# Reordering the opening of an attention and Fourier-mix kernel: sums ahead of products, short extra products, one load on another queue, weight conversions at other places

## The chip, the cores and the metric

The kernel runs on one core of a Trainium2 chip. The metric is device time in microseconds (us) of one execution. A core has five engines that matter here, each with its own instruction queue worked off in order: TensorE (PE), VectorE (DVE), ScalarE (ACT), GpSimd (POOL) and SyncE (SP), which here only issues loads and stores (DMAs). ScalarE can issue DMAs too.

## The reference

Eight batches, each with eight heads, a sequence of 576 and 64 elements per head (512 in all). Softmax over the elements of each query and over the sequence of each key; key-value products; queries times these give `x`. Then a Fourier mix, a normalisation and a two-layer MLP of width 2048 with a residual:

```
q_s = softmax(q, axis=-1);  k_s = softmax(k, axis=seq)
kv  = einsum('bhsd,bhse->bhde', k_s, v)
x   = einsum('bhsd,bhde->bhse', q_s, kv)      # joined to (B, S, 512)
u   = x + real(fft(fft(x, axis=seq), axis=512))
un  = (u - mean(u)) / sqrt(var(u) + 1e-6)
out = u + relu(un @ w1) @ w2
```

All inputs are f32, and the weights come as 64-bit words.

## The kernel before

**Batches.** For each batch the keys' exponentials are transposed on TensorE and multiplied with the values into block-diagonal 128x128 blocks (`kvr`). Queries come in tiles of 128 rows. Four such tiles of batch 0 are called A, B, D and C in the opening; the 64 rows of a batch that fill no tile of their own are handled with those of another batch as a "shared" tile `t`. A query tile is exponentiated, transposed (`turn`), copied, and multiplied with `kvr` to give `x`. The mix folds `x` by symmetry (`folded`, L936 to L956, on VectorE), multiplies the folds with tables `ft` (`block`, L988 and L991), then with `cd` (`second`, L1016 and L1019), adds, normalises, transposes (L1096) and lays the result out for the MLP (L1104).

**Stages.** From 0 to 56 us the opening runs attention and mix of batch 0 and the key products of batch 1. From 56.05 us the MLP of batch 0 runs as plain products (`plain`: 16 blocks of four 128x512 products at L1150, then 64 products at L1162). Beside it each piece of weights is converted from its words, in steps called hi, shift, sign, lo and add: two on ScalarE (L368, L369), two on VectorE (L362, L365), one on GpSimd (L370). Eight pairs of pieces per layer are then combined by four subtractions or additions on VectorE (`combine`, L420) and stored, and batch 1's attention, folds and mix are made ready. From 195.69 us on, batches 1 to 7 and the shared rows go through an MLP in Strassen's form (L1224 and after); TensorE bounds that part.

**Order.** Nothing is scheduled by the machine's state. Each step has a time written by hand or computed from a formula, all steps are sorted by it, and each engine gets its instructions in that order. The times are no clock; only their order counts. The opening's times are in the string `OPENING`, where "k03 max" is the maximum of batch 0's fourth block of keys, "k0 last" and "k0 fifth" are the transposes of the keys' last 128 columns and their copy, "t exp0" to "t exp3" are two exponentials each of the shared rows, "A kv" the products of tile A with `kvr`, "b1 times" a block of the mix, "c0 hi" a step of the first conversion. The times of the later steps are at the end of the program, as offsets from `first` (47.8) and from `t`, which is `first + 56`.

**Loads.** `loads_first` issues the loads of the opening. ScalarE issues four loads of shared rows (L264); SP issues four blocks of keys (L274), the first queries (L283), then the four first rows of the shared tile (`shared_firsts`, L267, 8 KB), then values, queries, values, tables, and batch 1's keys and values. Each load has one of eight completion counters, taken in rotation, and waits for the earlier load on its counter to land.

**Sums of exponentials.** Batch 0's query tiles are normalised after the product. In `q_times_kv` four products of 128x8 with a matrix of ones (L874) give the sums, in the same step as the four products with `kvr` (L876); VectorE then adds an epsilon and inverts (L881, L882), and scales the product into `x` (L890).

Of the kernel before, what the change touches and what calls it, by code (L numbers as in the profile page):

```python
# [40 lines left out]
F32 = mybir.dt.float32  # L41
# [5 lines left out]
P = 128  # L47
# [35 lines left out]

DOWN = [(i, f) for n in range(4) for i in (2, 3, 0) for f in range(4 * n, 4 * n + 4)] + [(1, f) for f in range(NF)]
OPENING = """
5.20 k00 max, 6.00 k00 exp, 6.20 k01 max, 6.95 k00 turn, 7.00 k01 exp, 7.20 k02 max, 7.80 k00 four,
7.95 k01 turn, 8.00 t max, 8.30 k02 exp, 8.60 k03 max, 9.06 k01 four, 9.25 k02 turn, 9.56 k03 exp, 10.20 A max,
10.32 t exp0, 10.51 k0 last, 10.80 B max, 10.80 t exp1, 10.95 A less, 11.28 t exp2, 11.40 k0 fifth,
11.76 t exp3, 11.99 B less, 12.00 k0 inverse, 12.12 k03 turn, 12.24 A exp, 12.37 t inverse, 12.74 k02 four,
12.82 k00 kv, 13.24 k03 four, 13.37 t normal, 13.72 A turn, 13.74 B exp, 14.00 C max, 14.17 k01 kv,  # L90
14.32 A copy, 14.60 D max, 14.75 C less, 15.07 B turn, 15.52 t turn, 15.67 B copy, 15.79 D less, 16.10 k02 kv,
16.17 t copy, 16.67 C exp, 16.83 t fold, 17.15 k03 kv, 17.17 D exp, 18.05 C turn, 18.20 k0 scale0,
18.28 t join, 18.50 D turn, 18.65 k0 scale1, 19.10 A kv, 20.10 B kv, 20.25 A inverse, 20.25 D copy,
20.65 A out, 21.10 D kv, 21.25 C copy, 21.27 k10 max, 21.94 B inverse, 22.07 k10 exp, 22.10 C kv,
22.25 D inverse, 22.50 B out, 23.10 k10 turn, 23.12 D out, 23.55 t kv, 23.70 k10 four, 23.74 C inverse,
23.99 tokens1, 24.25 t parts, 24.61 C out, 25.23 columns1, 25.59 tokens0, 26.21 t folds, 26.96 columns0,
27.44 by1, 27.80 by0, 28.28 again0, 28.58 again1, 28.60 c0 hi, 29.08 tokens3, 29.18 b1 times, 29.25 c0 lo,
29.70 tokens2, 30.16 b0 times, 30.32 columns3, 30.38 b1 copies, 30.68 columns2, 31.14 b4 times, 31.16 by2,
31.36 b0 copies, 31.52 by3, 32.00 again2, 32.30 again3, 32.34 b4 copies, 32.80 k13 max, 32.90 b2 times,
33.47 c0 shift, 33.60 k13 exp, 33.88 b3 times, 34.17 c0 sign, 34.36 b2 copies, 34.77 k12 max, 34.86 k13 turn,  # L100
34.89 c0 add, 35.08 b3 copies, 35.44 k11 max, 35.63 k12 exp, 35.78 m1 times, 36.39 k13 four, 36.68 k12 turn,
36.89 m1 copy, 37.13 m0 times, 37.28 k12 four, 37.39 m1 sums, 37.78 k11 exp, 38.29 m1 add0, 38.54 m0 copy,
38.73 k11 turn, 38.89 roots, 38.97 m1 add1, 39.04 m0 sums, 39.18 k1 last, 39.84 k1 inverse, 40.04 s10,
40.19 k11 four, 40.27 m0 add1, 40.69 k1 fifth, 40.79 s11, 41.34 k10 kv, 41.57 m0 add0, 41.69 root1,
42.09 k11 kv, 42.25 scales1, 42.45 s00, 42.60 normal11, 42.84 k12 kv, 43.20 s01, 43.44 turn11, 43.95 normal10,
44.04 k13 kv, 44.10 root0, 44.30 laid11, 44.45 scales0, 44.64 turn10, 44.80 normal00, 44.80 normal01,
45.30 k1 scale0, 45.39 laid10, 45.55 turn01, 45.75 k1 scale1, 46.15 turn00, 46.30 laid01, 46.90 laid00"""
ATT_EPS = 1e-9
# [27 lines left out]
class _Block:  # L136
# [96 lines left out]
    def xshared(self, p):  # L233
        return self.xpart(B, p % 2, p // 2)

    def halves(self):
        return self.work.tile([P, 2 * NN], F32, tag="eo", name="eo", bufs=6)

    def loads_first(self, fetch):
# [45 lines left out]
        def second(r):  # L285
# [282 lines left out]
    def opening(self, fetch, converted):  # L568
# [22 lines left out]
        for n, it in own.items():  # L591
            named(f"{n} max,{n} less,{n} exp", self.q_exp_spread(it))
            named(f"{n} turn,{n} copy", self.q_turn(it))
            named(f"{n} kv,{n} inverse,{n} out", self.q_times_kv(it))
        for name, f in zip(("tokens", "columns", "by", "again"), self.folded(0)):
# [20 lines left out]
        assert not steps, steps  # L616
        return placed

# [242 lines left out]
    def q_times_kv(self, it):  # L861
        nc, (_, b, c, u) = self.nc, it
        box = []

        def times():
            qT, *rec = self.live.pop(it)
            px = self.acc((P, D))
            box.extend([px, *rec])
            if b == 0:
                n = {(0, 0): "bb", (1, 1): "bc", (0, 1): "ba", (1, 0): "bb"}[c, u]  # L870
                t = self.ps.tile([P, 512], F32, tag=n, name=n)
                box.append(t)
                for r in range(NR):
                    nc.tensor.matmul(t[:, 0:H], lhsT=qT[:, r, :], rhs=self.ones[:, r, :], start=r == 0, stop=r == NR - 1)  # L874
            for r in range(NR):
                nc.tensor.matmul(px[:, r * P:(r + 1) * P], lhsT=qT[:, r, :], rhs=self.kvr[b % 2][:, r, :], start=True,  # L876
                                 stop=True)

        def inverse():
            t = self.small.tile([P, H], F32, tag="qrec", name="qrec", bufs=4)  # L880
            nc.vector.tensor_scalar(out=t[:], in0=box[1][:, 0:H], scalar1=ATT_EPS, scalar2=None, op0=ALU.add)  # L881
            nc.vector.reciprocal(t[:], t[:])  # L882
            box[1] = t[:].unsqueeze(2).to_broadcast([P, H, DH])
# [601 lines left out]
def kernel(ctx: ExitStack, tc: tile.TileContext, q, kT, v, w1, w2, ft,  # L1485
# [68 lines left out]
    steps.append((t + 12, lambda: setattr(blk, "spare_words", blk.raws[LATE_WORDS[0]].bitcast(F32))))  # L1554
    steps += [(t + 12 + 4 * i, lambda i=i: blk.load(i)) for i in range(3)] + [(t + 71, lambda: blk.load(3))]
# [8 lines left out]
    for k, dt in zip((2, 3, 0, 1, 4), (24.5, 26, 29, 30.5, 32)):  # L1564
        steps += at(t + dt, blk.block(1, k))
    for i, some in enumerate((blk.mix_own(1, 0), blk.mix_own(1, 1), blk.mix_shared(0))):
        steps += at(t + 35 + 3.4 * i, some)
    steps += at(t + 47, blk.norm(1)) + at(t, blk.ahead(2))

# [65 lines left out]
```

## Time and profile before

| what | value |
|---|---|
| time, median of 3 runs (lowest, highest) | 1094.94 us (1094.49, 1095.25) |
| the profiled execution: its time, its span | 1095.45 us, 1093.6 us |
| mean granted clock of TensorE | 0.994 |
| first MLP product (L1150) | 56.05 us |
| first Strassen product (L1224) | 195.69 us |

The span is the part of the execution that the trace covers, from the first instruction to the last; 1.85 us lie outside it. Starts of instructions are counted from the span's start. The profile's page cuts the span in 40 slices and gives each engine's busy share; a timeline lists runs of like instructions with start, duration and, in brackets, the idle time before them and what ended it; a table by windows gives each engine's busy time in chosen stretches with the clock granted to TensorE as a share of its full speed. A form such as `acc<-ft,eo 128*128 128x144` names the output and the inputs of a product with their sizes.

### The profile page before, as it was taken

How to read it: one execution, taken by the hardware profiler on the slowest of the kernel's cores; microseconds unless marked ns; L12 is line 12 of the kernel's file. 1: busy time of each engine (PE TensorE's matmuls, PEld its weight loads, DVE VectorE, ACT ScalarE, POOL GpSimd, SP SyncE). 2: the span in 40 equal slices, each digit the busy share in tenths (PEclk: the TensorE clock that was granted, in tenths of full speed). 3: DMA queues.
4: the chain of work that ended last, by engine and by line, in shares of the span. 5: the costliest groups of instructions: out<-in, count | busy, mean ns of one | idle time of the engine just before them, and what ended most of it. 6: DMA issues, size and time to landing. Idle time of an engine off the chain costs nothing.

```text
span 1093.6 us, 16946 instructions
## 1 busy us (share of the span) xinstructions
PE 1058.9 (97%) x6360; PEld 921.1 (84%) x6360; DVE 665.7 (61%) x1285; ACT 405.1 (37%) x962; POOL 459.9 (42%) x376
## 2 busy tenths in 40 slices
PE   6899889999999999999999999999999999999997
PEld 6744455888888899889998999889988998899896
DVE  4878776466545775757654775687547743562261
ACT  5685623452135314442344224521552132131200
POOL 3164210128323536255533742464435363554343
PEclk9999989999999999999999999999999999999999
DMA  9577577446998557555766576557744574576463
GB/s 299 197 244 275 173 273 236 152 147 217 300 337 261 174 192 261 193 188 193 246 232 211 174 245 205 209 199 242 240 164 154 195 255 166 200 246 219 164 241 125
DMA packets 114912, 236.41 MB, mean 216 GB/s; under 512 B 24320, under 2 KB 76288, under 8 KB 104208
## 3 DMA queue, kind: packets, MB, share of 16 engines
q1 hardware_dynamic: 113032, 234.29, 62.9%
q10 hardware_dynamic: 1800, 1.05, 0.3%
q8 instruction: 50, 0.82, 0.3%
q14 instruction: 30, 0.25, 0.1%
HBM read 200.18 MB, written 39.32 MB: 219 GB/s over the span
## 4 chain that ended last, share of the span: by engine, by line
PE 83%; DVE 4%; ACT 2%; issue 1%; POOL 1%; DVEq 0%; ACTq 0%; POOLq 0%
PE bb L1224 15%; PE bb L1350 10%; PE bc L1224 9%; PE ba L1224 9%; PE bc L1350 6%; PE ba L1350 6%; PE bb L1320 4%; PE acc L707 2%; PE acc L876 2%; PE bb L1435 2%; PE bc L1162 2%; PE acc L988 2%; PE acc L991 2%; PE acc L1016 1%; PE tr L1096 1%; PE bc L1435 1%
## 5 line engine op out<-in xcount | busy, mean ns | idle before, releaser
L1224 PE MATMUL bb<-unT,big 128*128 128x256 f32 x768 | 183.9, 380 | 0.0
L376 POOL TENSOR_TENSOR big<-big 128x512 f32<-128x512 f32 x32 | 40.9, 1278 | 285.9 <-ACT big L1236 285.9
L1224 PEld LDWEIGHTS bb<-unT,big 128*128 128x128 f32 x768 | 143.0, 190 | 18.4 <-DVE u L1194 0.4
L1236 ACT ACTIVATE big<-big 128x512 f32<-128x512 f32 x96 | 60.4, 629 | 199.7 <-DVE big L1235 199.5
L1194 DVE TENSOR_TENSOR u<-bb,s 128x512 f32<-128x512 f32 x66 | 45.6, 691 | 132.4 <-PE bb L1224 113.9
L1224 PE MATMUL bc<-unT,big 128*128 128x256 f32 x512 | 124.0, 380 | 0.0
L1224 PE MATMUL ba<-unT,big 128*128 128x256 f32 x512 | 123.8, 379 | 0.0
L1350 PE MATMUL bb<-big 128*128 128x128 f32 x848 | 105.2, 276 | 2.2 <-DVE u L1357 2.2
L1224 PEld LDWEIGHTS ba<-unT,big 128*128 128x128 f32 x512 | 94.8, 190 | 12.3 <-issue 0.5
L1224 PEld LDWEIGHTS bc<-unT,big 128*128 128x128 f32 x512 | 94.5, 190 | 12.1 <-DVE big L1235 0.6
L1350 PEld LDWEIGHTS bb<-big 128*128 128x128 f32 x848 | 99.6, 192 | 2.9 <-DVE u L1357 2.9
L1296 DVE TENSOR_TENSOR big<-big 128x512 f32<-128x512 f32 x92 | 82.9, 944 | 5.9 <-POOL big L377 3.4
L1300 POOL TENSOR_TENSOR x<-x,big 128x512 f32<-128x512 f32 x52 | 68.0, 1317 | 28.0 <-ACT big L1327 14.8
L1350 PE MATMUL ba<-big 128*128 128x128 f32 x640 | 79.6, 275 | 0.0
L1350 PEld LDWEIGHTS ba<-big 128*128 128x128 f32 x640 | 76.4, 192 | 1.2
L760 ACT ACTIVATE q<-q,qm 128x64 f32<-128x64 f32 x240 | 65.2, 338 | 27.9 <-DVE qm L754 22.6
L1296 POOL TENSOR_TENSOR big<-big 128x512 f32<-128x512 f32 x26 | 41.2, 1594 | 74.2 <-DVE big L1296 53.8
L1357 DVE TENSOR_TENSOR u<-bb,s 128x256 f32<-128x256 f32 x40 | 16.9, 422 | 70.5 <-PE bb L1350 61.8
L1320 PE MATMUL bb<-big 128*128 128x256 f32 x256 | 58.7, 381 | 0.0
L1235 DVE TENSOR_TENSOR big<-bc,u 128x512 f32<-128x512 f32 x64 | 43.9, 686 | 23.7 <-PE bc L1224 22.6
L1320 PEld LDWEIGHTS bb<-big 128*128 128x128 f32 x256 | 48.3, 190 | 7.9 <-DVE big L1235 1.1
L1350 PE MATMUL bc<-big 128*128 128x128 f32 x416 | 51.5, 275 | 0.0
(257 smaller groups left out, 2020.4 us busy)
## 6 DMA issues: line engine op xcount, KB each, us to landing
big<-w2d SPq DMA_DIRECT2D x67, 1024.0 KB, 4.9
big<-w1s SPq DMA_DIRECT2D x64, 896.0 KB, 5.1
big<-w2s SPq DMA_DIRECT2D x16, 1024.0 KB, 6.4
big<-in_w_dram SPq DMA_DIRECT2D x21, 512.0 KB, 6.3
w2d<-big SPq DMA_DIRECT2D x42, 256.0 KB, 5.9
q<-in_q_dram SPq DMA_DIRECT2D x27, 256.0 KB, 6.4
k<-in_kT_dram SPq DMA_DIRECT2D x24, 288.0 KB, 6.3
v<-in_v_dram SPq DMA_DIRECT2D x24, 256.0 KB, 4.7
```

What stands on the lines that cost most here:

```text
L376: e1.tensor_tensor(out=to(4), in0=at(2), in1=at(3), op=ALU.add)
L707: nc.tensor.matmul(pk, lhsT=ks[:, c, :], rhs=v[:, c, :], start=(c == 0), stop=(c == NC - 1))
L760: nc.scalar.activation(q[:, h, :], q[:, h, :], ACT.Exp, bias=m[:, h:h + 1])
L1194: plus = lambda t: V.tensor_tensor(out=temp(t), in0=box["bb"][:], in1=box["s1"][:], op=ALU.add)
L1224: nc.tensor.matmul(bank()[:, i, :], lhsT=w[:, WA_AT[m], k * P:(k + 1) * P], rhs=self.unT[g][:, B_AT[m], k, :], start=first and i == 0 and ...
L1235: steps = [(0, lambda: V.tensor_tensor(out=hp(i), in0=bank()[:], in1=u()[:], op=ALU.add)), (0.8, lambda: nc.scalar.activation(hp(i), hp(i) ...
L1236: (0.8, lambda: nc.scalar.activation(hp(i), hp(i), ACT.Relu))]
L1296: e.tensor_tensor(out=to(o), in0=to(x), in1=to(y), op=op)
L1300: G.tensor_tensor(out=x, in0=x, in1=tile(m), op=ALU.add)
L1320: nc.tensor.matmul(box[name][:, i, :], lhsT=h[p][:, A_AT[m], i * P:(i + 1) * P], rhs=self.stream[n][:, p, :], start=p == 0 and (m != 1 or ...
L1350: nc.tensor.matmul(box[place[n]][:, i, :], lhsT=own(m)(A_AT[n])[:, f, :], rhs=w[:, r // 2, r % 2 * P:r % 2 * P + P], start=first and f == ...
L1435: nc.tensor.matmul(bank()[:, i, :], lhsT=h[p][:, A_AT[m], i * P:(i + 1) * P], rhs=w[:, p, :], start=first and i == 0 and p == 0, stop=p == ...
```

## The change

1. `shared_firsts`, the 8 KB load, is issued by ScalarE instead of SP, at 8.3 in the order, that is between the exponentials of k02 and k03.
2. The fifth block of batch 0's values is loaded for 64 rows only; a memset on GpSimd fills the other 64 with zeros.
3. `q_times_kv` is split: a step "ones" with the products with ones, ahead of "kv".
4. A method `warm` issues products of 128x256 (identity times `kvr` of batch 1) into bank `ba`, and nobody reads their result. Fifteen of them are placed at seven places of the opening.
5. `OPENING` is written anew. Among others, k03's maximum comes ahead of t's; t's maximum and exponentials come after k03's exponential and A's and B's maxima; D's tile is before C's; tokens2 is earlier; k10 and k11 are both exponentiated before the tokens; batch 1's `k1 inverse` and scales stand at the end, after the products of its keys, which stand before the norm's transposes.
6. The conversions, the combinations and batch 1's steps beside the MLP of batch 0 have new times. In before, conversions 26 to 31 stand at `t` + 0, 13, 15.5, 18, 20.5 and 23; now the last sixteen stand at `first` + 27 to 49 and at `t` - 2, 3, 8, 12, 15, 17.2, 29, 32, 35 and 38, the last four of them behind batch 1's folds (at `t` + 19.5). All line numbers behind the edits shift by 8 to 13; L876 becomes L888.

```diff
+WARM = (3, 3), (8.1, 1), (10.85, 1), (26.6, 2), (29, 3), (41.3, 3), (42.8, 2)
 OPENING = """
-7.95 k01 turn, 8.00 t max, 8.30 k02 exp, 8.60 k03 max, 9.06 k01 four, 9.25 k02 turn, 9.56 k03 exp, 10.20 A max,
...
+7.25 k01 turn, 7.60 k03 max, 7.65 k02 exp, 8.41 k01 four, 8.60 k02 turn, 8.91 k03 exp, 9.50 A max,
+9.67 k02 four, 9.86 k0 last, 10.10 B max, 10.25 A less, 10.36 k03 turn, 10.70 k0 fifth, 11.01 k03 four,
+11.29 B less, 11.30 k0 inverse, 11.50 t max, 11.51 A exp, 11.60 k00 kv, 12.25 A turn, 12.25 t exp0,
+12.70 k01 kv, 12.73 t exp1, 13.21 t exp2, 13.40 D max, 13.69 t exp3, 14.00 C max, 14.15 D less, 14.17 B exp,
...
+    def warm(self, n):
+        t = self.ps.tile([P, 512], F32, tag="ba", name="ba")
+        for _ in range(n):
+            self.nc.tensor.matmul(t[:, 0:2 * P], lhsT=self.ident[:], rhs=self.kvr[1][:, 0:2, :], start=True, stop=True)
...
         def shared_firsts():
-            load(tail[0:P:Q], self.q[b:b + 2].rearrange("b s n -> (b s) n")[::S // 2])
+            nc.scalar.dma_start(tail[0:P:Q], self.q[b:b + 2].rearrange("b s n -> (b s) n")[::S // 2])
...
-            load(v[:, 4, cols], self.v[b, S - P:, cols])
+            load(v[64:, 4, cols], self.v[b, 512:, cols])
...
-        order = [shared, table, *(lambda r=r: keys(r) for r in range(NR)), lambda: queries(0), shared_firsts,
+        order = [lambda: nc.gpsimd.memset(v[0:64, 4, :], 0.0), shared, table, *(lambda r=r: keys(r) for r in range(NR)), lambda: queries(0),
...
-        return [(i / 100, step) for i, step in enumerate(order)]
+        return [(8.3, shared_firsts)] + [(i / 100, step) for i, step in enumerate(order)]
...
+        def ones():
+            qT = self.live[it][0]
+            n = {(0, 0): "bb", (1, 1): "bc", (0, 1): "ba", (1, 0): "bb"}[c, u]
+            box.append(self.ps.tile([P, 512], F32, tag=n, name=n))
+            for r in range(NR):
+                nc.tensor.matmul(box[0][:, 0:H], lhsT=qT[:, r, :], rhs=self.ones[:, r, :], start=r == 0, stop=r == NR - 1)
...
-        return [(0, times), (1, inverse), (1.3, out)] if b == 0 else [(0, times), (1.3, out)]
+        return [(0, ones), (0, times), (1, inverse), (1.3, out)] if b == 0 else [(0, times), (1.3, out)]
...
-    first, second, both = 47.8, 56, 77
+    first, second, both = 48.2, 56, 77
...
-    for i in range(1, 2 * NF - 6):
-        steps += at(first - (1.9 if i == 1 else 0.8) + 1.7 * (i - 1) if i < NF else first + 26 + 3 * (i - NF), converted(i))
-    for p, dt in enumerate((15, 20, 25, 35.5, 39, 42.5, 57, 61)):
-        steps += at(first + dt, combined(0, p))
...
-    for i, dt in zip(range(2 * NF - 6, 2 * NF), (0, 13, 15.5, 18, 20.5, 23)):
-        steps += at(t + dt, converted(i))
+    words = [first - 1.9, *(first + 0.9 + 1.7 * i for i in range(NF - 2))]
+    words += [first + dt for dt in (27, 31, 35, 39, 44, 49)] + [t + dt for dt in (-2, 3, 8, 12, 15, 17.2, 29, 32, 35, 38)]
+    for i, dt in enumerate(words, 1):
+        steps += at(dt, converted(i))
+    for p, dt in enumerate((15, 20, 25, 36, 41, 46.5, 59, 62.5)):
+        steps += at(first + dt, combined(0, p))
...
-    for p, dt in zip((3, 0, 1, 7, 2, 4, 5, 6), (28, 31, 34, 37, 46, 53, 58, 63)):
+    for p, dt in zip((3, 0, 1, 7, 2, 4, 5, 6), (30.5, 33.5, 37, 45, 50, 56, 61, 65)):
...
-        steps += at(at_q + 9, blk.q_turn(it)) + at(at_q + 13.5, blk.q_times_kv(it))
-    steps += at(t + 11, blk.t_times_kv(1)) + at(t + 19, blk.folded(1))
+        steps += at(at_q + 9.5, blk.q_turn(it)) + at(at_q + 14, blk.q_times_kv(it))
+    steps += at(t + 11, blk.t_times_kv(1)) + at(t + 19.5, blk.folded(1))
```

More of the change, by code (lines that the diff above doesn't have):

```diff
@@ L84 @@
 DOWN = [(i, f) for n in range(4) for i in (2, 3, 0) for f in range(4 * n, 4 * n + 4)] + [(1, f) for f in range(NF)]
+WARM = (3, 3), (8.1, 1), (10.85, 1), (26.6, 2), (29, 3), (41.3, 3), (42.8, 2)
 OPENING = """
-5.20 k00 max, 6.00 k00 exp, 6.20 k01 max, 6.95 k00 turn, 7.00 k01 exp, 7.20 k02 max, 7.80 k00 four,
-7.95 k01 turn, 8.00 t max, 8.30 k02 exp, 8.60 k03 max, 9.06 k01 four, 9.25 k02 turn, 9.56 k03 exp, 10.20 A max,
-10.32 t exp0, 10.51 k0 last, 10.80 B max, 10.80 t exp1, 10.95 A less, 11.28 t exp2, 11.40 k0 fifth,
@@ L89 @@
[L89 to L107, printed above, removed]
+4.50 k00 max, 5.30 k00 exp, 5.50 k01 max, 6.25 k00 turn, 6.30 k01 exp, 6.50 k02 max, 7.15 k00 four,
@@ new lines @@
+7.25 k01 turn, 7.60 k03 max, 7.65 k02 exp, 8.41 k01 four, 8.60 k02 turn, 8.91 k03 exp, 9.50 A max,
+9.67 k02 four, 9.86 k0 last, 10.10 B max, 10.25 A less, 10.36 k03 turn, 10.70 k0 fifth, 11.01 k03 four,
+11.29 B less, 11.30 k0 inverse, 11.50 t max, 11.51 A exp, 11.60 k00 kv, 12.25 A turn, 12.25 t exp0,
+12.70 k01 kv, 12.73 t exp1, 13.21 t exp2, 13.40 D max, 13.69 t exp3, 14.00 C max, 14.15 D less, 14.17 B exp,
+14.60 t inverse, 14.67 A copy, 14.82 B turn, 15.19 C less, 15.30 D exp, 15.32 A ones, 15.80 B copy,
@@ new lines @@
+16.12 k02 kv, 16.23 t normal, 16.34 C exp, 16.77 D turn, 16.85 A inverse, 17.22 t turn, 17.72 k03 kv,
+17.87 t copy, 18.37 B ones, 18.52 k0 scale0, 18.97 k0 scale1, 19.17 C turn, 19.32 B inverse, 19.62 A kv,
+19.72 t fold, 20.32 k10 max, 20.42 t join, 20.59 B kv, 20.72 D copy, 20.99 A out, 21.22 k10 exp, 21.56 D ones,
+21.98 C copy, 22.03 B out, 22.36 D kv, 22.65 D inverse, 23.05 k11 max, 23.33 C ones, 23.72 D out,
+23.85 k11 exp, 24.13 C kv, 24.34 C inverse, 24.74 tokens1, 25.10 k11 turn, 25.36 C out, 25.55 k10 turn,
@@ new lines @@
+25.70 k11 four, 25.98 columns1, 26.00 t kv, 26.20 k10 four, 26.34 tokens0, 26.96 tokens2, 27.05 t parts,
+27.58 columns0, 28.06 by1, 28.15 c0 hi, 28.42 by0, 28.78 t folds, 28.80 c0 lo, 29.53 again0, 29.83 again1,
+30.33 tokens3, 30.43 b1 times, 30.95 columns2, 31.31 columns3, 31.41 b4 times, 31.63 b1 copies, 31.79 by3,
+32.15 by2, 32.39 b0 times, 32.61 b4 copies, 32.63 again2, 32.93 again3, 33.43 k13 max, 33.53 b3 times,
+33.59 b0 copies, 34.10 c0 shift, 34.23 k13 exp, 34.51 b2 times, 34.80 c0 sign, 34.99 b3 copies, 35.40 k12 max,
@@ new lines @@
+35.49 k13 turn, 35.52 c0 add, 35.71 b2 copies, 36.26 k12 exp, 36.41 m0 times, 37.02 k13 four, 37.31 k12 turn,
+37.52 m0 copy, 37.76 m1 times, 37.91 k12 four, 38.02 m0 sums, 38.66 k1 last, 38.86 m1 copy, 38.92 m0 add0,
+39.26 k1 fifth, 39.60 m0 add1, 39.60 m1 sums, 39.76 roots, 39.91 k10 kv, 40.40 s00, 40.66 k11 kv,
+40.90 m1 add1, 41.15 s01, 41.41 k12 kv, 42.05 root0, 42.16 k13 kv, 42.20 m1 add0, 42.88 scales0, 43.08 s10,
+43.23 normal01, 43.83 s11, 43.98 turn01, 44.58 normal00, 44.73 root1, 44.93 laid01, 45.08 scales1,
@@ L108 @@
+45.23 turn00, 45.43 normal10, 45.43 normal11, 45.98 laid00, 46.08 turn10, 46.68 turn11, 46.83 laid10,
+47.43 laid11, 49.00 k1 inverse, 49.30 k1 scale0, 49.60 k1 scale1"""
 ATT_EPS = 1e-9
@@ L593, in opening @@
             named(f"{n} turn,{n} copy", self.q_turn(it))
-            named(f"{n} kv,{n} inverse,{n} out", self.q_times_kv(it))
+            named(f"{n} ones,{n} kv,{n} inverse,{n} out", self.q_times_kv(it))
         for name, f in zip(("tokens", "columns", "by", "again"), self.folded(0)):
@@ L616, in opening @@
         assert not steps, steps
+        for t, n in WARM:
+            placed.append((t, lambda n=n: self.warm(n)))
         return placed
@@ L867, in times @@
             px = self.acc((P, D))
[L868 to L874, printed above, removed]
+            box.insert(0, px)
+            box.extend(rec)
             for r in range(NR):
@@ L880, in inverse @@
             t = self.small.tile([P, H], F32, tag="qrec", name="qrec", bufs=4)
-            nc.vector.tensor_scalar(out=t[:], in0=box[1][:, 0:H], scalar1=ATT_EPS, scalar2=None, op0=ALU.add)
+            sums = box.pop()
+            nc.vector.tensor_scalar(out=t[:], in0=sums[:, 0:H], scalar1=ATT_EPS, scalar2=None, op0=ALU.add)
             nc.vector.reciprocal(t[:], t[:])
-            box[1] = t[:].unsqueeze(2).to_broadcast([P, H, DH])
+            box.append(t[:].unsqueeze(2).to_broadcast([P, H, DH]))
         def out():
@@ L1550 @@
         steps += at(t + 1.2 * i, some)
[L1551 to L1552 removed]
+    words = [first - 1.9, *(first + 0.9 + 1.7 * i for i in range(NF - 2))]
[4 more added lines that the diff above has]
+        steps += at(first + dt, combined(0, p))
     steps += [(t + 0.5 + 0.1 * i, lambda i=i: fetch(i)) for i in LATE_WORDS]
[L1554 to L1556 removed]
+    steps.append((t + 6, lambda: setattr(blk, "spare_words", blk.raws[LATE_WORDS[0]].bitcast(F32))))
+    steps += [(t + 14 + 4 * i, lambda i=i: blk.load(i)) for i in range(3)] + [(t + 71, lambda: blk.load(3))]
+    for p, dt in zip((3, 0, 1, 7, 2, 4, 5, 6), (30.5, 33.5, 37, 45, 50, 56, 61, 65)):
         steps += at(t + dt, combined(1, p))
@@ L1561 @@
         steps += at(t - 34 + i if i < 3 else t + 0.6, blk.q_load(it)) + at(at_q, blk.q_exp(it))
-        steps += at(at_q + 9, blk.q_turn(it)) + at(at_q + 13.5, blk.q_times_kv(it))
-    steps += at(t + 11, blk.t_times_kv(1)) + at(t + 19, blk.folded(1))
-    for k, dt in zip((2, 3, 0, 1, 4), (24.5, 26, 29, 30.5, 32)):
+        steps += at(at_q + 9.5, blk.q_turn(it)) + at(at_q + 14, blk.q_times_kv(it))
+    steps += at(t + 11, blk.t_times_kv(1)) + at(t + 19.5, blk.folded(1))
+    for k, dt in zip((2, 3, 0, 1, 4), (25, 26.5, 29.5, 31, 32.5)):
         steps += at(t + dt, blk.block(1, k))
     for i, some in enumerate((blk.mix_own(1, 0), blk.mix_own(1, 1), blk.mix_shared(0))):
-        steps += at(t + 35 + 3.4 * i, some)
-    steps += at(t + 47, blk.norm(1)) + at(t, blk.ahead(2))
+        steps += at(t + 35.5 + 3.4 * i, some)
+    steps += at(t + 47.5, blk.norm(1)) + at(t, blk.ahead(2))
     scale, before = 0.87, t + both
```

## The prediction

> **What bounds the kernel now.** I read the page first. Its table of busy time says that TensorE is the bound: 97% of the span. The gain to be had is therefore the time in which TensorE stands or runs at half clock, and the slices (27 us each) say where: the first two and the fourth or fifth.
>
> ```profile
> PE 1058.9 (97%) x6360; PEld 921.1 (84%) x6360; DVE 665.7 (61%) x1285; ACT 405.1 (37%) x962; POOL 459.9 (42%) x376
> PE   6899889999999999999999999999999999999997
> ```
>
> From 195.69 us (the first L1224 product) to the end TensorE works without gaps, and the change leaves the order of every engine's instructions there alone. So I measure two distances: start to first MLP product (L1150, 56.05 us), and that to 195.69.
>
> Next the timeline of TensorE, where brackets give the stall ahead of an entry and who ended it. The opening first:
>
> ```profile
> 13.13 1.11 PE L530 MATMUL tr<-ident,big 128*128 128x128 f32 x4 [0.79 <-DVE big L541]
> 14.04 1.91 PE L552 MATMUL acc<-big,ks 128*128 128x128 f32 x8
> ...
> 35.32 1.12 PE L988 MATMUL acc<-ft,eo 128*128 128x144 f32 x4 [3.88 <-issue]
> ...
> 56.05 1.53 PE L1150 MATMUL ba<-unT,big 128*128 128x512 f32 x3 [1.52 <-ACT unT L1104]
> ```
>
> From 14.04 to 31.45 TensorE is full, then waits 3.88 us for the DVE's folds, which end at 35.5. The second stretch:
>
> ```profile
> 109.63 0.63 PE L816 MATMUL tr<-ident,q 128*128 128x128 f32 x4 [1.85 <-DVE q L788]
> ...
> 121.96 1.16 PE L876 MATMUL acc<-kvr,qT 128*128 128x128 f32 x8 [1.20 <-ACT qT L826]
> ...
> 125.42 0.63 PE L816 MATMUL tr<-ident,q 128*128 128x128 f32 x4 [1.44 <-issue]
> ...
> 144.51 0.59 PE L988 MATMUL acc<-ft,eo 128*128 128x144 f32 x2 [2.46 <-DVE eo L956]
> 146.03 0.85 PE L988 MATMUL acc<-ft,eo 128*128 128x145 f32 x2 [0.93 <-DVE eo L956]
> ```
>
> With 0.57 and 0.41 us that the same view has between them, these stalls are 8.86 us. Last the windows by stage, for the granted clock (the first of a row's last three numbers; the other two are the DMA share and GB/s):
>
> ```profile
> 35.50:38.90 3.40, 3.40 (x12) 2.97 (x12) 3.30 (x10) 0.55 (x3) 0.00 (x0) 0.50 1.08 372
> 148.20:151.60 3.40, 3.40 (x9) 2.30 (x8) 3.26 (x8) 0.32 (x4) 1.34 (x1) 0.50 0.01 3
> ```
>
> The clock halves after each of the long stalls: 3.4 us behind the 3.88 us one, 6.8 us (144.75 to 151.6) behind the 2.46 us one. A pair of L1162 takes 1.92 us there against 1.02 elsewhere, four L988 1.17 against 0.66. Work of those windows, halved: 1.7 us in the opening, about 2.9 us in the second.
>
> **Part 1, shared rows on ScalarE's queue.** In SP's timeline the fifth load is issued at 4.24 and the next (L267, the 8 KB rows) only at 7.52: it waits for ScalarE's four loads of shared rows, and everything behind it with it. Then its landing at 9.48 lets the DVE run "t max", and behind that in the DVE's queue stands "k03 max", whose keys had landed at 7.69:
>
> ```profile
> 9.56 0.69 DVE L754 TENSOR_REDUCE qm<-big 128x8 f32<-128x512 f32 x1 [2.02 <-DMA big<-in_q_dram]
> 10.16 0.74 DVE L522 TENSOR_REDUCE km<-big 128x1 f32<-128x576 f32 x1
> ```
>
> After, k03 max stands first (7.7), its exponential follows k02's (7.91 + 0.97 = 8.9) instead of starting at 10.94: 2.0 us earlier. Everything up to the first kv product (14.04) hangs on that; with the ScalarE copies between, 1.6 us come through: 12.4. The 8 KB load now sits on ScalarE between k02's and k03's exponential. It costs 0.46 us of issue there (four took 1.83), and as loads share eight rotating completion counters it also waits for the first query load (landed 8.89 before). So it goes out at about 8.9. Behind it on ScalarE: k01's copy, k03's exponential; and behind its landing the eight t exponentials (2.00 us), and behind those B's exponential and copies; on the DVE t max now stands ahead of C and D max. SP meanwhile has put out 1.8 MB, from about 4.7 on. Bounds for the landing: 1.96 us after issue (its own row before, 7.52 to 9.48, little else queued), or behind all 1.8 MB, at 370 GB/s 4.9 us and more: about 14 to 15. The nearest row is the start, where ScalarE's second load landed at 5.30 and SP's second at 5.58: neither queue waited for the other. The Trainium skill ("DMA: Bandwidth & Descriptors", Queues, rings and completion order) says that an engine takes turns between the queues, packet by packet; elsewhere the page says that spreading loads over issuing engines gives no bandwidth. That second rule speaks against the move, and I agree: no byte comes sooner for it, what it buys is SP's 2.9 us. By the first rule and the row I take 2 to 3.5 us, landing by 12.4, which t max at its new place (after A and B max, k0 fifth) barely feels. The half load (64 rows of values) saves 0.13 MB, under 0.4 us of queue, hidden; the memset on GpSimd is before any use, hidden.
>
> **Part 2, order of the opening.** The sums of exponentials (L874, 0.48 us a set) go ahead of the kv products, so the inverse (0.37 us on the DVE) is ready before the product. The last of the four x ends in before at 30.84, 0.7 us after its product. Sum: 1.6 us from the start, about 0.7 us from inverse and out: first L988 at about 33.0 instead of 35.32. From there to the first MLP product it is 20.7 us now; the half clock of 1.7 us should go, and of the stalls of 0.32, 0.87 and 1.52 us some: k1's kv products move ahead of the norm.
>
> **Part 3, short products.** 15 of 128x256. L1150 takes 0.86 us for 128x512, so 0.43 each, 0.86 cold. The first five lie before TensorE has anything, or in its waits (1.28 and 0.79 us at 11.86 and 13.13); five (29.1 to 30.9) lie in the hole ahead of L988. The last five are in a full stretch: 5 x 0.43 = 2.15 us on the path, unless they fall in its 2.7 us of waits. So: minus 1.7, plus 2.15, minus some of 2.7: about 0 to -0.5. Opening in sum: -2.4, first MLP product at 53.6. Will they warm the clock? Before, the clock is at half until 18.46 (four transposes 1.11 us, later 0.60). The skill ("TensorE: Matmul & The Clock Gate", Part 4) says that transposes do not count as busy for the gate. The trace neither shows nor denies it: the window that raised the clock (15.04 to 18.46) holds 0.85 us of transposes and 2.6 of products; the one before it, mostly transposes, did not. By the rule the window 11.6 to 15.04 of after again holds too little, and the clock rises at 18.46 as before; if transposes count, at 15.04, some 1.5 us better. I take the rule and leave 1.5 us in the range.
>
> **Part 4, conversions spread.** A conversion is two ScalarE operations (0.57 each), two on the DVE (L362 0.42, L365 0.69) and an add on GpSimd (L370, 1.3 to 1.4). None is removed. In before, four stand among batch 1's folds (132 to 148), and each costs more than itself, since DVE operations that overlap GpSimd's add stretch until it has ended:
>
> ```profile
> 135.02 1.36 POOL L370 TENSOR_TENSOR big<-big,spare 128x512 int32<-128x512 int32 x1 [11.75 <-ACT spare L369]
> 144.06 1.43 POOL L370 TENSOR_TENSOR big<-big,spare 128x512 int32<-128x512 int32 x1 [2.38 <-DVE eo L955]
> ```
>
> ```profile
> 135.26 1.67 DVE L365 SCALAR_TENSOR_TENSOR big<-spare,big 128x512 int32<-128x512 int32 x1
> 144.28 1.37 DVE L955 TENSOR_TENSOR eo<-eo 128x128 f32<-128x128 f32 x1
> ```
>
> Against 0.69 and 0.28 these two lose 2.1 us; L936's pair (2.42 against 1.29) and L942's (1.84 against 0.84) 2.1 more. With 4 x 1.1 us of the conversions' own, the fold chain (133.15 to 145.97, 12.8 us) shrinks to about 4.2. After, the last four stand behind the folds (t + 29 and later against folds at t + 19.5), so the stall of 3.39 us goes nearly whole, and the half clock of 2.9 us behind it. The 5.47 us before are ScalarE and DVE queues with conversions, combinations and exponentials in a row; spread and with q's turn 0.5 later, most goes. At most 8.86 + 2.9 = 11.8 us. But what is late next is the DVE: it is busy 41.6 of the 50 us from 104 to 154 (windows); less 4.2 of stretching, 37.4 would have to fit in some 40. I keep 5 of the 11.8 for new stalls: -6.6.
>
> **Sum.** 1095.45 (the profiled execution: span 1093.6 and 1.85 around it) - 2.4 - 6.6 = 1086.4. The profiled run is 0.5 above the median of the runs: 1085.9, rounded to 1086.0.
>
> **Rivals.**
> 1. The rows land late, behind SP's loads (14 to 15 us). For: 1.8 MB queued. Against: the side-by-side landings above. ScalarE then runs t's exponentials to 16.5 and B's after 16.5, where before it started at 15.09; the opening ends about 2.5 us later than before, at 58.5: 1095 + 2.5 - 6.6 = 1091. Chance 0.16.
> 2. The stalls go whole and the clock stays up: -11.8 of part 4, -2.4, less 1.3 for the x of the last q that the folds still need: 1082. Chance 0.12. Against: the DVE's 37 of 40 us.
> 3. The spreading only moves the stalls (the sum of the DVE's work stays, collisions with GpSimd too): opening alone, 1095 - 2.4 = 1092.5. Chance 0.12.
> 4. Slower: the rows land later still and hold ScalarE. Each us past 12.4 costs about one, as B's exponential, both copies and so A, B, D and C wait behind t. If spreading gives 6.6, the loss begins when the rows land 9 us late, after the tables (landed at 18.25 and 19.08 before); if it gives nothing, from 15 on. Landing at 22 with a third of the spreading: +7 - 2, 1099. Chance 0.04.
>
> The likeliest case, 1083.5 to 1088.5, has 0.53; 0.03 is left for no change. 0.2% (2.2 us) is about what a measurement of this kernel can tell from none. Faster 0.93, same 0.03, slower 0.04. Range 1081.8 to 1092.2: it takes in rivals 1, most of 2 and half of 3.
>
> **What would show it.** First kv product (L552) at 12.4, first L988 at 33 without 0.50 in the clock behind it, first L1150 at 53.6, first L1224 at 186 to 187; no L365 or L936 over 1.3 us among the folds. I am wrong if the rows land after 12.5, if the last short products push the first L1150, or if stalls of over 1.5 us stand ahead of L816 or L988 again.

## The result, and the profile after

The changed kernel takes 1088.43 us (median of 4 runs, 1087.04 to 1089.42), the kernel before 1095.1 us beside it. The ratio is 0.9937, with a 95% interval of 0.9920 to 0.9954: about 7 us, or 0.6%, faster. The profiled execution took 1088.17 us, its span is 1086.4 us. The forecast was 1086.0 in a range of 1081.8 to 1092.2.

The page's first row, against 1058.9 busy us before: TensorE's busy time has grown by 5 us, while the span has shrunk by 7.2. (By their starts the short products take about 8.6 us; less work at half clock takes a part of that back.)

```profile
PE 1063.9 (98%) x6390; PEld 922.5 (85%) x6390; DVE 667.9 (61%) x1285; ACT 405.4 (37%) x962; POOL 461.0 (42%) x377
```

TensorE's timeline in the opening (L538, L560, L1001 and L1163 are L530, L552, L988 and L1150 of before; L242 are the short products):

```profile
12.82 1.06 PE L242 MATMUL ba<-kvr,ident 128*128 128x256 f32 x2
13.67 1.41 PE L560 MATMUL acc<-big,ks 128*128 128x128 f32 x8
...
34.12 0.76 PE L1001 MATMUL acc<-ft,eo 128*128 128x144 f32 x4 [0.98 <-DVE eo L968]
...
54.59 5.37 PE L1163 MATMUL ba<-unT,big 128*128 128x512 f32 x8 [1.51 <-ACT unT L1117]
59.79 3.60 PE L1163 MATMUL bb<-unT,big 128*128 128x512 f32 x8
```

The first MLP product starts 1.46 us earlier than before (54.59 against 56.05). But its block of four products takes 5.2 us until the next block starts, where before it took 3.5 (56.05 to 59.56). At the second block nothing is left of the gain. The windows of the changed kernel say why; the clock is the first of the last three numbers:

```profile
51.95:55.40 3.45, 1.47 (x6) 0.91 (x7) 2.28 (x6) 3.45 (x7) 0.91 (x1) 1.00 0.00 0
55.40:58.80 3.40, 3.40 (x5) 1.35 (x4) 2.88 (x5) 0.69 (x2) 1.66 (x2) 0.50 0.45 154
```

A stretch in which TensorE was busy 1.47 of 3.45 us is followed by 3.4 us at half clock: 1.7 us lost. In the second stretch, the stalls that are left:

```profile
127.03 1.13 PE L888 MATMUL acc<-kvr,qT 128*128 128x128 f32 x8 [1.13 <-DVE big L373]
...
129.57 0.63 PE L826 MATMUL tr<-ident,spare 128*128 128x128 f32 x4 [0.55 <-issue]
...
140.52 0.95 PE L1001 MATMUL acc<-ft,eo 128*128 128x144 f32 x4 [1.70 <-DVE eo L969]
```

With two of 0.18 and 0.17 us they are 3.73 us instead of 8.86, and none is followed by half clock. That is 5.1 us of stalls and the 2.9 us of half clock, 8.0 in sum, against 7.8 measured in this stretch. So, stage by stage, by the starts of products:

| stage | before, us | after, us | difference |
|---|---|---|---|
| start to second MLP block | 59.56 | 59.79 | +0.23 |
| second MLP block to first Strassen product (188.13) | 136.13 | 128.34 | -7.79 |
| first Strassen product to the end of the span | 897.91 | 898.27 | +0.36 |

All of the gain is in the second stretch.

### The profile page after: what moved, and what is told of

Its sections match the earlier page's. It is cut to its first block, busy times and chain, and to the rows that moved or that the text cites. A ratio compares the mean times of both kernels' runs of the same rounds, so it can differ in the third digit from the quotient of the medians.

```text
span 1086.4 us, 16999 instructions
## 1 busy us (share of the span) xinstructions
PE 1063.9 (98%) x6390; PEld 922.5 (85%) x6390; DVE 667.9 (61%) x1285; ACT 405.4 (37%) x962; POOL 461.0 (42%) x377
## 4 chain that ended last, share of the span: by engine, by line
PE 83%; DVE 5%; ACT 2%; issue 1%; POOL 1%; DVEq 0%; ACTq 0%; POOLq 0%
PE bb L1237 15%; PE bb L1363 10%; PE bc L1237 10%; PE ba L1237 10%; PE bc L1363 6%; PE ba L1363 6%; PE bb L1333 4%; PE acc L717 2%; PE acc L888 2%; PE bb L1448 2%; PE bc L1175 2%; PE acc L1001 2%; PE acc L1004 2%; PE acc L1029 1%; PE bc L1448 1%; PE ba L1448 1%
## 5 line engine op out<-in xcount | busy, mean ns | idle before, releaser
L1237 PEld LDWEIGHTS ba<-unT,big 128*128 128x128 f32 x512 | 94.7, 190 | 12.4 <-issue 0.5
```

The lines of the kernel that those rows point to most:

```text
L1237: nc.tensor.matmul(bank()[:, i, :], lhsT=w[:, WA_AT[m], k * P:(k + 1) * P], rhs=self.unT[g][:, B_AT[m], k, :], start=first and i == 0 and ...
```

## The experiments

All were timed beside the kernel before. The starts and half clocks are those of the one profiled execution; the ratios are of the medians of 4 to 13 executions. Where the intervals of two runs overlap, their ratios alone do not tell them apart. "Second block" is the second MLP block, "Strassen" the first product of that part.

| run | ratio to before (95% interval) | first MLP product | second block | Strassen | half clock behind 20 us |
|---|---|---|---|---|---|
| before | 1 | 56.05 | 59.56 | 195.69 | 35.5 to 38.9, 144.8 to 151.6 |
| changed | 0.9937 (0.9920 to 0.9954) | 54.59 | 59.79 | 188.13 | 55.4 to 58.8 |
| open_only | 1.0002 (0.9994 to 1.0010) | 54.56 | 59.74 | 195.14 | 54.5 to 57.9, 146.7 to 150.1 |
| later_only | 0.9938 (0.9925 to 0.9950) | 55.61 | 59.11 | 186.78 | 32.8 to 39.6 |
| last_four | 0.9955 (0.9939 to 0.9971) | 55.73 | 60.94 | 191.20 | 35.4 to 38.8, 55.9 to 59.3 |
| one_less | 0.9915 (0.9899 to 0.9931) | 54.14 | 58.07 | 186.02 | none (11.5 to 14.95 ahead of it) |
| no_warm | 0.9918 (0.9904 to 0.9931) | 52.66 | 57.86 | 186.19 | 32.5 to 35.9, 53.0 to 56.4 |
| rows_sp | 0.9922 (0.9909 to 0.9934) | 53.26 | 58.42 | 186.68 | 53.2 to 56.6 |
| rows_early | 0.9936 (0.9921 to 0.9952) | 56.15 | 61.35 | 189.72 | 56.7 to 60.1 (8.9 to 15.7 ahead of it) |
| warm_end | 0.9926 (0.9910 to 0.9942) | 55.08 | 59.04 | 187.23 | none |
| all_fifteen | 0.9910 (0.9895 to 0.9926) | 53.90 | 57.83 | 185.57 | none (17.4 to 20.8 ahead of it) |
| holes_only | 0.9889 (0.9875 to 0.9902) | 51.51 | 55.48 | 183.20 | none |
| none_at_all | 0.9907 (0.9893 to 0.9921) | 50.77 | 54.71 | 182.43 | none |
| acc_later | 0.9892 (0.9875 to 0.9908) | 51.89 | 55.86 | 183.99 | none |

**Which half of the change gains: open_only and later_only.** One has the new opening and the old block of conversions, combinations and batch 1's steps (at its old offsets from `first`), the other the reverse.

```diff
 open_only: all of the change, but behind "first, second, both = 48.2, 56, 77" the lines of before
 later_only: the kernel before, but behind "first, second, both = 47.8, 56, 77" the changed lines
```

> The new opening with the old places of conversions, combinations and batch 1's steps. Theory (the gain lies in the second stretch; the opening's 1.5 us are eaten by the half clock of 55.4 to 58.8 us in the first MLP block): within 1 us of the kernel before, 1094 to 1096; first MLP product at about 54.6, second block at about 59.8 (before 59.56); stalls of 2.5 us at the folds of batch 1 as before. Rival (the opening gives what was forecast, the half clock is a chance of one execution): 1092.5 or less, with the second MLP block at 58 or earlier.

> The old opening with the new places of conversions, combinations and batch 1's steps. Theory: nearly the whole gain, 7 to 8 us, so 1087 to 1088; no half clock in 130 to 155 us. Rival (opening and spreading share the gain as forecast, 2.4 and 6.6 less what was missed): 1089.5 to 1090.

The opening alone changes nothing that can be measured (0.9994 to 1.0010), and the later part alone gives as much as the whole (0.9938 against 0.9937). So the gain lies in the second stretch, and the rival, that the two halves share it, falls.

**Which conversions: last_four and one_less.**

```diff
 last_four, against before:
-(0, 13, 15.5, 18, 20.5, 23)      (28, 31, 34, 37, 46, 53, 58, 63)
+(0, 13, 29, 32, 35, 38)          (30.5, 33.5, 37, 45, 50, 56, 61, 65)
 one_less, against the changed kernel:
-(-2, 3, 8, 12, 15, 17.2, 29, 32, 35, 38)
+(-2, 3, 8, 12, 28, 17.2, 29, 32, 35, 41)
```

> The kernel before with one thing changed: its last four conversions stand behind batch 1's folds (and the combinations of the second layer, which need those pieces, at the changed kernel's places). Theory (each conversion among the folds costs its own 1.1 us on the DVE and about 1 us of stretching beside GpSimd's add, and the stall is followed by half clock): the 3.4 us of stall ahead of L988 shrink to under 1, no half clock at 145 to 152, time -5 to -6 us (1089). Rival (the spreading earlier, from 104 to 127 us, carries half): stall gone but stalls elsewhere grow, time -3 us or less.

From the second block to the first Strassen product it takes 130.26 us against 136.13: -5.87, in the theory's interval. In before, the pair of L942 among the folds looked like this:

```profile
140.13 1.84 DVE L942 TENSOR_TENSOR eo<-eo 128x255 f32<-128x255 f32 x2
```

In last_four no conversion stands among the folds, and the last GpSimd add ends at 137.74:

```profile
138.65 0.69 DVE L936 TENSOR_TENSOR eo<-x 128x512 f32<-128x512 f32 x1 [2.06 <-ACT x L892]
139.26 0.75 DVE L942 TENSOR_TENSOR eo<-eo 128x255 f32<-128x255 f32 x2
```

L942's pair takes 0.75 us, and VectorE even waits 2.06 us for the `x`. Its stalls of 1.58, 0.58, 0.41, 1.20 and 1.42 us between 110 and 127 us stand as in before; the folds' products follow theirs without one. So of the 7.8 us some 5.9 come from the four conversions (and the combinations that follow them). The rest, by subtraction, belongs to the spreading ahead of them; no run has that alone.

> The changed kernel with conversion 26 too moved behind the folds (and 31, which takes over its buffer, 3 later). Theory (the 1.70 us ahead of the folds' first product in the changed kernel is the two conversions that still stand there, 132.7 to 135.9 us on the DVE, and their adds on GpSimd): that stall shrinks by 1.1 to 1.7, time -1 to -1.7 us. Rival (the folds wait for the x of the last query tile, copied at 134.6 to 135.1, so the stall stays): within 0.5 us of the changed kernel.

The stall of 1.70 us at the folds is gone, as the theory said, but the stretch is only 0.39 us shorter (127.95 against 128.34). Further down TensorE's timeline has it back:

```profile
171.50 0.66 PE L1109 MATMUL tr<-ident,eo 128*128 128x128 f32 x4 [1.31 <-ACT eo L1103]
```

VectorE is 9.79 and 9.83 of 10 us busy in the windows from 150 to 160 and 160 to 170 of this run (9.90 and 9.86 in the changed kernel), so a wait taken out ahead of them comes back behind them. What one_less has better than the changed kernel in its profiled execution is mostly the half clock that it does not have at 55. Theory and rival were both wrong: the stall went, and the time came back later.

**The short products: no_warm.** `WARM = ()`.

> The changed kernel without the fifteen short products. Theory (they bring the clock up at 14.4 instead of about 18, and hold it across the hole ahead of the folds' products at 30 to 34): clock at half until about 18 us and again for 3.4 us after 34; first MLP product 1.5 to 2.5 us later than 54.6, time +1 to +2.5 us (1089.5 to 1091). Rival (they cost as much as they bring: five of them, 2.15 us, lie on the path behind 45.5): first MLP product at 54.6 +- 0.7 and the time within 1 us of the changed kernel.

The theory falls. The half clock at 32.5 is there as expected, but the first MLP product is 1.93 us earlier, not later, and the clock comes up at 11.99 instead of 14.4. The ratio is lower than the changed kernel's, though the intervals overlap. Two things came together. Taking the products out moved the order in which the loads get their counters (so I read it), and the 8 KB load no longer waited for the first queries: ScalarE issued it at 7.41 instead of 8.86, and t max started at 12.36 instead of 14.10, 1.74 us earlier. That is a second edit that I had not meant; it points to the rows. The products themselves come out even: from t max to the folds' first product it takes 20.07 us without them and 20.02 with them, and from there to the first MLP product 20.23 us (32.43 to 52.66) against 20.47, although 1.7 us go to half clock. So they cost about what they brought, as the rival had it.

**The 8 KB rows: rows_sp and rows_early.**

```diff
 rows_sp:
-            nc.scalar.dma_start(tail[0:P:Q], ...
+            load(tail[0:P:Q], ...
-  lambda: queries(0), lambda: values(0)          [(8.3, shared_firsts)] + [...]
+  lambda: queries(0), shared_firsts, lambda: values(0)      [...]
 rows_early:
-  lambda: queries(0), lambda: values(0)          [(8.3, shared_firsts)] + [...]
+  shared_firsts, lambda: queries(0), lambda: values(0)      [...]
```

> The changed kernel with the 8 KB load of shared rows back on SP's queue at its old place. Theory (on ScalarE's queue the 8 KB landed at 14.1, behind the loads SP had put out; on SP's it stands first): rows land at about 9.5, the t exponentials start about 1 us earlier than 14.8, values and queries land 2 to 3 us later; the two nearly cancel, first MLP product at 54 to 55.5, time within 1 us of the changed kernel. Rival (the move is what the opening lives on): first MLP product at 56 or later, time +1.5 to +3.

In the changed kernel ScalarE issues the load at 8.86, and VectorE's t max waits for it until 14.10, 5.2 us later (ScalarE's issue, then VectorE):

```profile
8.86 1.13 ACTq L275 DMA_DIRECT2D big<-in_q_dram  x1
```

```profile
14.10 0.69 DVE L764 TENSOR_REDUCE qm<-big 128x8 f32<-128x512 f32 x1 [1.04 <-DMA big<-in_q_dram]
```

In rows_sp, on SP's queue, t max starts at 12.38 without waiting:

```profile
12.38 0.69 DVE L764 TENSOR_REDUCE qm<-big 128x8 f32<-128x512 f32 x1
```

And this although values and second queries are issued about 4 us later (the second queries keep VectorE waiting 2.09 us, to 15.16). The first MLP product is 1.33 us earlier. This is more than the theory allowed, and the rival is refuted: undoing the move costs nothing and, in the profiled execution, helps. (The ratios, 0.9922 and 0.9937, are not apart by their intervals.)

> The changed kernel with the 8 KB load of shared rows still on ScalarE's queue, but put out right behind the keys' loads, ahead of the queries, instead of behind k02's exponential. Theory (in the changed kernel the rows land 5.2 us after their issue, at 14.1, since SP has 2 MB of loads in front, and t's exponentials, then B's, hang on that): issue at about 4, landing by 8.5, t's exponentials at about 13.1 instead of 14.8, first MLP product 1 to 1.5 us before 54.6, time -1 to -1.5 us (1087). Rival (the opening is set by TensorE's own work ahead of 14 us, short products among it): first MLP product at 54.3 or later, time unchanged.

This did not test what it was meant to test, but it is instructive. The load overlaps, by the rows it writes, with ScalarE's four loads of the same tile, and waits for all of them: it went out at 7.78, not 4, and held ScalarE's first exponential until 8.95:

```profile
8.95 0.77 ACT L533 ACTIVATE big<-big,km 128x576 f32<-128x576 f32 x1 [4.84 <-DMA big<-in_q_dram]
```

That is 3.9 us later than in the changed kernel (5.07), yet the first MLP product is only 1.56 us later, and t max 1.45 us (15.55). Six runs with the short products of the change agree in one distance, whichever engine issues the load: from t max to the first MLP product they take 40.49 (changed), 40.49 (open_only), 40.88 (rows_sp), 40.60 (rows_early), 40.46 (warm_end, with three products more) and 40.49 us (one_less). So the start of t max sets the opening. When the clock comes up does not matter to it: in open_only it was up at 6.7 us and in the changed kernel at 14.4, and both have their first MLP product at 54.6. It matters when the clock falls again behind t max: all_fifteen below, with the opening of rows_sp, takes 42.15 us, with half clock from 17.4 to 20.8.

**The half clock at the first MLP block: warm_end.** `(46.7, 3)` added to `WARM`.

> The changed kernel with three more short products, between the norm's last transposes and the first MLP product, where TensorE waits 1.51 us. Theory (the half clock that begins at 53 to 55 us in every kernel with the new opening comes from a window of 3.4 us that holds only transposes and waits, 0.4 busy, where the old opening had 0.55): no half clock after 50, the first MLP block takes 3.5 us instead of 5.2, time -1.5 to -1.7 us (1086.8). Rival (the three products don't keep the clock up, or push the first MLP product): time unchanged or up to 1 us more.

```profile
53.44 1.46 PE L242 MATMUL ba<-kvr,ident 128*128 128x256 f32 x6
55.08 3.67 PE L1163 MATMUL ba<-unT,big 128*128 128x512 f32 x8 [0.18 <-ACT unT L1117]
```

The stall of 1.51 us is filled and no half clock follows; the first block takes 3.96 us (0.29 of it a wait for GpSimd) instead of 5.20. In this execution the mechanism holds. But its mean clock was 0.999, and the three others of the run had 0.995, 0.997 and 0.997 (the changed kernel had 0.997 in all four, with one half clock where it was profiled): they lost clock somewhere that no trace shows. The time is 1.2 us lower by the ratios, which the intervals do not separate. One clause of the expectation is wrong: last_four, with the old opening, has the half clock at 55.9 too, and one_less, with the new one, does not. Of the profiled executions without these three products, five of eight with the new opening have a half clock that begins between 53 and 57 us, and one of three with the old; of the three with them (warm_end, holes_only, acc_later) none has.

**Which short products pay: all_fifteen, holes_only, none_at_all.** All three have rows_sp's and one_less's edits.

```diff
 all_fifteen: WARM as in the change
 holes_only:  WARM = (26.6, 2), (29, 3), (46.7, 3)
 none_at_all: WARM = ()
```

> The changed kernel with two edits that each helped alone: the 8 KB load back on SP's queue, and conversion 26 behind the folds; all fifteen short products kept. Theory (the two gains add: 1.3 us in the opening, 1.7 to 2 ahead of the folds): first MLP product at about 53.3, no stall ahead of L1001 at 138, time 3 to 4 us below the changed kernel, ratio to before 0.990 to 0.991. Rival (the DVE fills the gap with another wait): ratio 0.992 or more.

> As all_fifteen, but of the short products only the five in the wait ahead of the folds' products (30 us), and three more in the wait ahead of the first MLP product. Theory (the ten others lie on TensorE's path or bring nothing: about 2.15 us behind 44 us, up to 1 us ahead of 13; the eight hold the clock at two places where it would fall): first MLP product at 51 to 52, no half clock behind 35 us, time 2.5 to 4 us below all_fifteen. Rival (the ones at the start set the clock up early and pay for themselves): within 1 us of all_fifteen.

> As all_fifteen, without any short product. Theory (they cost 2.15 us on the path and save 1.7 of half clock at 32 to 36; the half clock at 53 to 57 comes either way): 0.5 to 1 us below all_fifteen, two half clocks of 3.4 us, 1.7 to 3 us above holes_only. Rival (the short products are worth their price): above all_fifteen by 1 us or more.

holes_only has the lowest ratio of all: 1083.05 us, its runs (1082.40 to 1083.21) all below those of all_fifteen (1084.30 to 1086.40), 2.3 us between the medians of these two, which ran beside each other; the theory had said 2.5 to 4. The first MLP product is 2.4 us earlier. The first products of the folds divide that up (rows_sp, all_fifteen, holes_only):

```profile
32.79 0.76 PE L1001 MATMUL acc<-ft,eo 128*128 128x144 f32 x4 [0.98 <-DVE eo L968]
```

```profile
33.42 0.76 PE L1001 MATMUL acc<-ft,eo 128*128 128x144 f32 x4 [0.98 <-DVE eo L968]
```

```profile
32.41 0.76 PE L1001 MATMUL acc<-ft,eo 128*128 128x144 f32 x4 [0.98 <-DVE eo L968]
```

From there to the first MLP product it takes 20.47, 20.48 and 19.10 us: the five products behind 44 us cost 1.4. From t max to there it takes 20.41, 21.67 and 20.48 us: the first five cost nothing that shows, and all_fifteen has lost 1.3 us to its half clock from 17.4 to 20.8.

The runs of none_at_all teach most: one took 1082.23 at a mean clock of 0.999 (the profiled one, with no half clock at all, where two were expected), the four others 1084.47 to 1086.15 at 0.995 or 0.996. holes_only has 0.998 or 0.999 in every run. The median of none_at_all is 0.6 us above that of all_fifteen, where 0.5 to 1 below was expected by the theory and 1 or more above by the rival; neither is borne out. So the eight products in the holes gain nothing on an execution that is lucky with the clock and 1.4 to 3.1 us on the four others, as far as five executions can tell; of the other ten, five cost 1.4 us and five bring nothing. all_fifteen came out 3 us below the changed kernel by the ratios, as expected, but its profile shows the same 1.3 us before the norm's transposes that one_less has.

**A last wait: acc_later.** In holes_only, `12` becomes `13.5` in the list of conversions.

> As holes_only, with conversion 25 moved from t + 12 to t + 13.5, behind the x copy of batch 1's third query tile. Theory (the 1.13 us that TensorE waits ahead of L888 at 122, ended by the DVE's L373, is a wait for a bank: a conversion keeps one of the three acc banks that the query products take in turn): that stall goes or falls below 0.3, time -0.8 to -1.1 us below holes_only, near 1082. Rival (the bank goes to another and the wait only moves to the next query product or to the folds): same time, and a stall of like size within 10 us behind.

```profile
122.35 1.13 PE L888 MATMUL acc<-kvr,qT 128*128 128x128 f32 x8 [1.13 <-DVE big L373]
124.89 0.63 PE L826 MATMUL tr<-ident,spare 128*128 128x128 f32 x4 [0.55 <-issue]
```

```profile
125.25 0.66 PE L826 MATMUL tr<-ident,spare 128*128 128x128 f32 x4 [1.86 <-DVE spare L798]
```

The first two lines are holes_only, the third acc_later. The stall of 1.13 us goes, as the theory had it, but the next grows from 0.55 to 1.86 us, so the rival is right about the time (ratios 0.9889 and 0.9892). VectorE is 9.33 of 10 us busy from 110 to 120 and again from 120 to 130; moving one wait makes another.

## Why the prediction was right, and where it was wrong

**The sum** was -9.0 us, measured are -7.2 in the span. That the sum came so near is in part luck: two errors stood against each other, 2.6 us too much hoped for from the opening and 1.2 too little from the conversions. All three of the signs that I had named for being wrong came true: the rows landed at 14.1, short products push the first MLP product (1.4 us by holes_only), and a stall of 1.70 us stands ahead of the folds' first product. Two conversions are left ahead of the folds, with an L373 (L365 of before) of 1.69 us and a pair of L949 (L936) of 2.37 us.

**Part 4, the conversions (-6.6): the mechanism right, the size a little too small.** Measured -7.8. The fold chain shrank as worked out (last_four: no stall, no half clock, -5.87), and of the 11.8 us at most 4.0 were kept, where I kept 5. The reason for keeping them was also right: VectorE is the next bound (44.8 of the 50 us from 104 to 154 in the changed kernel), and one_less and acc_later show stalls that mostly move.

**Part 1, the landing of the rows: wrong.** I took 2 to 3.5 us for the 8 KB, landing by 12.4; they took 5.2 and landed at 14.1. That was the upper of my two bounds. I chose the row of the start (5.30 beside 5.58), where both queues had just begun, over the 1.8 MB that SP had put out by then. The rule of turns between the queues did not help: this load of 8 KB in four rows took as long as 1.97 MB, which is what the queues moved between its issue and its landing, with some 2 MB outstanding when it went out (the sizes of the loads issued by then, less the 2.26 MB moved). Why the turns did not help, no run shows. What I had said hangs on the rows, that each us of delay past 12.4 costs one, was right (40.5 us from t max to the first MLP product). Undone alone (rows_sp), the step is worth 1.3 us at the first MLP product.

The load also held ScalarE longer than the 0.46 us that I had put down: k02's exponential was done at 8.49, the issue waited until 8.86, when the first queries had landed, and took 1.13 us. k01's copy and k03's exponential stood behind it:

```profile
10.03 0.59 ACT L541 COPY ks<-tr 128x512 f32<-128x512 f32 x1 [1.54 <-PE tr L538]
10.51 0.78 ACT L533 ACTIVATE big<-big,km 128x576 f32<-128x576 f32 x1
```

So k03's exponential started at 10.51 instead of 8.9, and the first product of keys and values at 13.67 instead of 12.4.

**Part 2, the order: not tested alone.** The folds' first product came at 34.12 us, 1.2 us earlier than before instead of the 2.3 forecast. No run takes out the sums that stand ahead of the products, or the half load.

**Part 3, the short products: wrong in two terms.** "The first five lie before TensorE has anything, or in its waits": of those, the one at 12.82 stands between k03's transposes and the first kv product and takes 0.85 us there, and that at 8.11 stands ahead of k02's transposes. No run shows a loss by it at the folds. And the half clock that I credited (-1.7, the window behind the wait for the folds) was saved, but the same loss came back at 55.4: I had not asked what TensorE does between the norm's transposes and the first MLP product once batch 1's key products no longer lie among them. (The old opening can meet it too: last_four.) The last five cost 1.4 us, inside what I allowed. With this the opening, forecast at -2.4, came to +0.2 at the second MLP block.

**The rule on transposes**: I took the Trainium skill's word ("TensorE: Matmul & The Clock Gate", Part 4) that they do not count for the clock. no_warm's trace speaks against it. Its clock rose at 11.99 (by the durations, and six times 3.41 us ahead of its fall at 32.47), after this window, in which transposes (L538, L546) ran until 11.4 and products only in the last 0.6 us. If the products alone counted, that would be less than the 1.47 of 3.45 us at which the changed kernel's clock fell. (The clock column reads 1.00 here although the clock is at half: the profile does not show the half clock of the start. I read it from durations, four transposes in 1.11 us before the rise and 0.66 behind it.)

```profile
8.60:12.00 3.40, 3.40 (x15) 2.52 (x14) 2.43 (x5) 2.19 (x5) 2.04 (x2) 1.00 1.07 388
```

**The rivals.** Rival 1 (rows late, opening 2.5 us later than before) had the landing right (14 to 15) and its effect too large: B's exponential started at 16.74 as it said, but the first MLP product came at 54.59 and not at 58.5. Rival 3 fell with later_only, rival 2 with VectorE's load.

## What to carry to other kernels

Ask of each piece of filler work whether it lies in a wait or in front of something: short products in two holes gained 1.4 to 3.1 us on four of five executions, five in a full stretch cost 1.4, and five at the start brought nothing. A small load that many steps hang on belongs ahead of the large ones on the same queue; on another queue behind 2 MB it landed 5.2 us after its issue. When an engine's stalls are cut by spreading another engine's work, look how full that other engine is: beyond that the stalls only move.

## What was not expected of the hardware

The granted clock changes on a grid. In before it changed at 35.52, 38.94, 144.75 and 151.58 us, which is 1, 32 and 34 times 3.41 us behind the first; in no_warm at 32.47, 35.88, 52.95 and 56.37, which is 1, 6 and 7 times. So half clocks last 3.41 us or twice that. Where the grid lies differs from execution to execution: in kernels with the same start (three short products at 2.29 us) the clock came up, by the durations and the grid, at 5.4 (rows_sp), 6.7 (open_only), 8.1 (one_less), 14.4 (changed) and 15.1 us (warm_end). Nor does coming up early help for long: it fell again at 8.9 us in rows_early, at 11.5 in one_less and at 17.35 in all_fifteen.

A busy share does not decide alone. In all_fifteen TensorE was busy 2.28 of 3.4 us, with eight records of 128x8 products among it, and the clock still fell at 17.35:

```profile
13.90:17.30 3.40, 2.28 (x20) 2.19 (x20) 3.20 (x6) 3.04 (x8) 2.04 (x2) 1.00 1.01 382
17.30:20.80 3.50, 3.50 (x19) 3.50 (x18) 0.86 (x3) 0.75 (x2) 0.28 (x1) 0.51 1.11 373
```

In before it stayed up over a step of its grid (five and six times 3.41 us behind 35.52: 52.59 to 56.00) with this as all but its whole work:

```profile
52.60 1.94 PE L1096 MATMUL tr<-ident,eo 128*128 128x128 f32 x12
```

What exactly is counted stays open.
